# Weights in another order, so that 48 modes are summed ahead of the tail, and a tail with 32-row spectra on four row groups and pairs of banks

## The chip, the cores and the metric

The kernel runs on one core of a Trainium2 chip. The metric is the device time of one execution in microseconds (us). Every time quoted comes from runs of the state "fast" (one single look, one_group, has no known state); a few tenths of a per cent matter here, so the experiments were timed in three or five rounds beside the kernel before. A ratio is the mean time of one kernel's fast runs over the mean of the other's fast runs in the same rounds, so it is not quite the ratio of the medians that are quoted with it. All kernels of one call shared a chip and the runs of the kernel before; the experiments came in four calls, on four chips.

PE is the matmul engine, DVE the vector engine, ACT the scalar engine, POOL a fourth engine that can also add, SP the queue that issues most output transfers. A bank is one PSUM accumulator of 128 x 512 f32 sums. The clock is the part of full speed that PE was granted (1.00 or 0.50 where it matters here), the share of transfers is the mean busy share of the 16 DMA engines.

## The reference, cut to what matters

```python
# attention: 8 batches, 8 heads, 576 rows, 64 columns; heads 0-3 a local mask, 4-7 a strided one
x = attention(q, k, v)                       # [8, 576, 512]
X = np.fft.rfft(x, axis=1)                   # 64 modes are kept
Yr = einsum('bmd,mde->bme', Xr, w_r) - einsum('bmd,mde->bme', Xi, w_i)
Yi = einsum('bmd,mde->bme', Xr, w_i) + einsum('bmd,mde->bme', Xi, w_r)
y = np.fft.irfft(Y, n=S, axis=1)
u = x + y
return (u + np.maximum(u @ w_ch, 0.0)).astype(np.float32)     # out [8, 576, 512], 9.44 MB
```

Each mode has its own two 512 x 512 matrices. 64 modes of them are 134 MB in HBM and half of that in the 16-bit form in which the kernel keeps them. Every output row needs every mode: the inverse transform is a matmul whose contracted dimension is (mode, real or imaginary), 128 rows in all.

## The kernel before

The weights stream in half modes (256 of 512 input rows), in pairs of modes; one half of all 64 modes comes first, beside the attention, then the other half, beside the products with `w_ch` and the transposes.

```python
    def w_fetch(n=1):
        for _ in range(n):
            i = len(w_tiles)
            if i >= 2 * NM:
                return
            half, m = 1 - i // NM, i % NM
            if i // 2 in GUEST:
                wt = big.tile([128, 2, 4, DM], F16, tag=GUEST[i // 2], name="wt")
            else:
                wt = pw.tile([128, 2, 4, DM], F16, tag="w", name="wt")
            for ri, src in enumerate((moe_w_r, moe_w_i)):
                dst = wt[ds(64 * ri, 64)]
                rows = src[m : m + 2, ds(256 * half, 256), :].rearrange(
                    "m (p c) e -> p m (c e)", c=4
                )
                dst = dst.rearrange("p m c e -> p m (c e)")


                ones = range(2)
                if ri and not m:
                    ones = [1]
                elif i < 2 * NM - 4:
                    nc.gpsimd.dma_start(dst, rows)
                    continue
                for j in ones:
                    nc.gpsimd.dma_start(dst[:, j], rows[:, j])
            w_tiles.extend((wt[:, 0], wt[:, 1]))
```

When a group of 16 modes is complete, its spectra (`yys`, 32 rows per batch, and `zzs`, their product with `w_ch`) are copied to rows 32g to 32g+31 of a 128-row tile. Once the last group (g = 3) is there, the tail begins. It has 36 units of 128 output rows, each with a bank `v` (input of the relu) and a bank `u` (the sum), and one matmul over all 128 rows of spectra:

```python
    def rows_of(b, t, acc, spectra, fresh):
        if t < 4:
            todo = [(out_cols(t), b)]
        else:
            todo = [(ds(576, 128), b - 1), (ds(512, 128), b)]
        for i, (cols, bb) in enumerate(todo):
            nc.tensor.matmul(
                acc,
                cs["cA"][:, cols],
                spectra[bb],
                start=fresh and i == 0,
                stop=(i == len(todo) - 1),
            )
```

The units of the tail (cut):

```python
    def v_rows(i):
        b, t = units[i]
        if i not in vps:
            v_early(i)
        vp = vps.pop(i)
        rows_of(b, t, vp, zzs, False)
        if t % 2 == 0:
            n = len(rls) // 2 % 2
            rl = ptr.tile([128, 2, 576], FP, tag="xT" if n else "rl", bufs=2, name="rl")
            rls[b, t] = rls[b, t + 1] = rl[:, :, 0:DM]
        rl = rls[b, t][:, t % 2, :]
        nc.scalar.activation(out=rl, in_=vp, func=ACTF.Relu)
        if pool_adds(b, t):
            nc.gpsimd.tensor_tensor(out=rl, in0=rl, in1=x_rows(b, t), op=AluOp.add)

    def u_early(i):
        b, t = units[i]
        ups[i] = psum("u")
        if not pool_adds(b, t):
            nc.tensor.matmul(ups[i], idn, x_rows(b, t), start=True, stop=False)

    def u_rows(i):
        b, t = units[i]
        if i not in ups:
            u_early(i)
        up = ups.pop(i)
        rows_of(b, t, up, yys, pool_adds(b, t))
        if t % 2 == 0:
            osbs[b, t] = osbs[b, t + 1] = pw.tile([128, 2, DM], FP, tag="w", name="osb")
        osb = osbs[b, t]
        halves = [ds(0, 256), ds(256, 256)] if i == LAST else [slice(None)]
        for cols in halves:
            nc.vector.tensor_tensor(
                out=osb[:, t % 2, cols],
                in0=up[:, cols],
                in1=rls[b, t][:, t % 2, cols],
                op=AluOp.add,
            )
        if t == 4:
            for j in range(2):
                (nc.scalar if b == B - 1 and j else nc.sync).dma_start(
                    out[b - 1 + j, ds(512, 64), :], osb[ds(64 * j, 64), 0, :]
                )
        elif i < 2 or i >= LAST - 1:
            for j, cols in enumerate(halves):
                (nc.scalar if i == LAST and j == 0 else nc.sync).dma_start(
                    out[b, ds(128 * (t - t % 2), 256), cols].rearrange(
                        "(p i) e -> p i e", i=2
                    )[:, t % 2, :],
                    osb[:, t % 2, cols],
                )
        elif t % 2:
            nc.sync.dma_start(
                out[b, ds(128 * (t - 1), 256), :].rearrange("(p i) e -> p i e", i=2),
                osb,
            )
    ...
    for m in range(END, NM):
        mode(1, m)
        if m < END + 2:
            for w in early[3 * (m - END) : 3 * (m - END) + 3]:
                w()
        else:
            again(0 if m < NM - 6 else 4 if m < NM - 2 else 2)
    spec_last(0)
    again(3)
    v_early(2, warm)
    spec_out(3, 0, *held[0])
    done = 0
    for i in range(len(units)):
        v_rows(i)
        b, t = units[i]
        if t == 1 and b + 1 < B:
            if b + 1 == 4:
                spec_last(1)
            spec_out(3, b + 1, *held[(b + 1) // 4])
        lag = 3 if 3 < i < LAST - 3 else 2
        while done <= i - lag:
            u_rows(done)
            done += 1
    while done <= LAST:
        u_rows(done)
        done += 1
    psum_pools()
```

The softmax here doesn't subtract the row's maximum and nothing guards it: scores larger than these inputs give would overflow.

## Time and profile before

| | before |
|---|---|
| median of 4 runs | 434.88 us (433.83 to 436.02) |
| span of the profiled run | 434.2 us |
| last weight matmul ends | 394.7 us |
| first add of the tail starts, last ends | 399.7, 428.4 us |
| output transfers flow | 401.3 to 431.5 us |

The prediction below shows the page, the stretches and the groups of this profile. Two more views serve the comparison. First the timeline of PE and DVE at the start of the tail (columns: start, us, engine, line, operation, output from inputs, shape, count, and the idle time ahead of it with what ended that).

```profile
394.08 0.64 PE L547 MATMUL y<-X,wt 128*128 128x16 f16 x16
395.30 1.91 PE L887 MATMUL y<-w_ch,YT 128*128 128x512 f16 x4
399.74 0.69 DVE L929 TENSOR_TENSOR osb<-u,rl 128x512 f32<-128x512 f32 x1 [0.28 <-ACT rl L908]
```

Four 512-column matmuls take 1.91 us at 395.3; at full clock they take 1.04 us (order_alone, below). The clock reads 0.50 from 395.0 to 397.3: PE runs them at half clock. Second, a stretch of 1 us in the tail (columns: busy PE, weight load, DVE, ACT, POOL; clock; transfer share; GB/s).

```profile
403.00:404.00 1.00, 1.00 (x7) 0.41 (x6) 0.84 (x2) 1.00 (x3) 1.00 (x2) 1.00 0.00 0
```

The transfer engines stand still for this 1 us (share 0.00, as at 411 to 412) while every compute engine works, so in the kernel before the tail is bound by compute more than by transfers.

### The profile page before, as it was taken

The page shows a single profiled execution, that of the slowest core. Times are in us where ns is not written, and L with a number is a line of the kernel's source. Part 1 is how long each engine was busy: PE and PEld are TensorE (multiplying, and loading weights), DVE is VectorE, ACT ScalarE, POOL GpSimd, SP SyncE. Part 2 cuts the span into 40 slices and gives each one's busy share as a digit, 9 for nine tenths or more (in the row PEclk, how much of TensorE's full clock was granted, in tenths as well). Part 3 has the DMA queues.
Part 4 walks back from the last instruction along what each step waited for, and adds up shares of the span by engine and source line. Part 5 has one row for each costly group of instructions (what it writes and reads, how often), then busy time and mean ns, then how long its engine had stood idle before and what let it go on. Part 6 is the DMA issues. An engine that isn't in the chain of part 4 may idle for free.

```text
span 434.2 us, 12103 instructions
## 1 busy us (share of the span) xinstructions
PE 338.5 (78%) x5307; PEld 244.5 (56%) x5307; DVE 215.9 (50%) x468; ACT 187.5 (43%) x352; POOL 129.3 (30%) x208
## 2 busy tenths in 40 slices
PE   1986888779985787889885566587789798968993
PEld 1865776658864575667753344454456465643441
DVE  2888678744433243342511033355436366503894
ACT  1686678634643435444440401143215123602892
POOL 6433332322332222222222222222222221200992
PEclk9999899865985859875865569887958899988999
DMA  8999999999999999999999999999999999991787
GB/s 176 210 211 213 214 212 213 211 211 213 213 212 212 214 214 212 214 214 213 214 212 213 213 214 214 212 214 215 211 214 214 212 214 214 213 182 30 272 330 261
DMA packets 29140, 92.18 MB, mean 212 GB/s; under 512 B 4064, under 2 KB 5344, under 8 KB 29088
## 3 DMA queue, kind: packets, MB, share of 16 engines
q0 software_dynamic: 24704, 81.28, 94.4%
q1 hardware_dynamic: 3584, 9.59, 5.9%
q8 instruction: 42, 0.69, 0.6%
q10 hardware_dynamic: 800, 0.54, 0.5%
q14 instruction: 10, 0.08, 0.0%
HBM read 163.22 MB, written 9.44 MB: 398 GB/s over the span
## 4 chain that ended last, share of the span: by engine, by line
DMA 68%; PE 19%; DVE 6%; ACT 2%; issue 2%; POOL 1%; DVEq 0%; POOLq 0%
DMA wt<-in_moe_w_i_dram 51%; DMA wt<-in_moe_w_r_dram 11%; DMA ring<-in_q_dram 5%; PE y L547 2%; PE v L689 2%; DVE xb L250 2%; DVE kz L292 2%; PE u L689 2%; PE v L895 2%; PE sc L514 1%; ACT X L260 1%; PE tp L395 1%; DVE rec L249 1%; PE sc L441 1%; PE sc L353 1%
## 5 line engine op out<-in xcount | busy, mean ns | idle before, releaser
L547 PE MATMUL y<-X,wt 128*128 128x16 f16 (+1 forms) x2048 | 82.4, 192 | 61.0 <-DMA wt<-in_moe_w_i_dram 59.4
L547 PEld LDWEIGHTS <-wt 128*128 128x128 f16 (+1 forms) x2048 | 72.9, 103 | 76.5 <-issue 68.5
L196 POOL DMA_DIRECT2D wt<-in_moe_w_r_dram x62 | 36.5, 589 | 141.7 <-PE y L547 67.4
L196 POOL DMA_DIRECT2D wt<-in_moe_w_i_dram x60 | 35.4, 590 | 73.5 <-DMA wt<-in_moe_w_i_dram 61.2
L654 ACT ACTIVATE v<-sc 128x512 f16<-128x512 f32 x32 | 19.1, 597 | 69.7 <-PE sc L645 69.6
L645 PE MATMUL sc<-w_cp,xT 128*128 128x512 f16 (+1 forms) x160 | 48.2, 430 | 0.0
L471 ACT ACTIVATE PL<-sc 128x480 f16<-128x480 f32 (+1 forms) x48 | 27.3, 580 | 46.8 <-PE sc L457 46.5
L655 DVE COPY xo<-tp 128x512 f16<-128x512 f16 x32 | 22.1, 692 | 35.7 <-PE tp L653 35.6
L249 DVE RECIPROCAL rec<-av 90x4 f32<-90x4 f32 (+2 forms) x80 | 14.7, 184 | 46.2 <-PE av L486 34.8
L250 DVE TENSOR_TENSOR xb<-av,rec 90x256 f16<-90x256 f32 (+2 forms) x80 | 36.0, 450 | 2.7
L402 DVE COPY qT<-tp 128x576 f16<-128x576 f16 x16 | 12.0, 758 | 38.8 <-PE tp L395 35.9
L260 ACT ACTIVATE v<-tp 128x640 f16<-128x640 f16 (+1 forms) x24 | 19.4, 808 | 24.9 <-PE tp L429 22.1
L395 PE MATMUL tp<-cI_s,ring 64*64 64x64 f16 x864 | 26.7, 213 | 0.8 <-DVE qT L402 0.6
L360 ACT ACTIVATE PL<-sc 90x360 f16<-90x360 f32 (+1 forms) x48 | 22.7, 491 | 6.1 <-PE sc L353 5.3
L929 DVE TENSOR_TENSOR osb<-u,rl 128x512 f32<-128x512 f32 (+1 forms) x37 | 23.7, 674 | 1.8 <-PE u L689 1.1
L395 PEld LDWEIGHTS <-ring 64*64 64x64 f16 x864 | 21.1, 125 | 5.7 <-issue 2.6
L910 POOL TENSOR_TENSOR rl<-rl,xo 128x512 f32<-128x512 f32 x16 | 18.3, 1157 | 18.2 <-ACT rl L908 17.9
L441 PE MATMUL sc<-cMl_s,cI_s 128*128 128x480 f16 (+1 forms) x48 | 22.5, 468 | 1.6 <-ACT X L260 1.6
L457 PE MATMUL sc<-qT,kz 128*128 128x160 f16 (+1 forms) x160 | 22.4, 267 | 0.0
L908 ACT ACTIVATE rl<-v 128x512 f32<-128x512 f32 x36 | 20.4, 600 | 4.7 <-PE v L689 3.9
L285 PE MATMUL tp<-cI_s,ring 72*128 72x72 f16 x256 | 15.1, 206 | 9.4 <-DMA ring<-in_v_dram 7.9
L260 ACT ACTIVATE kz<-tp 64x360 f16<-64x360 f16 (+1 forms) x32 | 19.1, 595 | 7.7 <-PE tp L395 6.1
(103 smaller groups left out, 655.7 us busy)
## 6 DMA issues: line engine op xcount, KB each, us to landing
wt<-in_moe_w_r_dram POOLq DMA_DIRECT2D x62, 512.0 KB, 19.0
wt<-in_moe_w_i_dram POOLq DMA_DIRECT2D x60, 512.0 KB, 19.4
out_dram<-osb SPq DMA_DIRECT2D x14, 512.0 KB, 2.7
ring<-in_v_dram POOLq DMA_DIRECT2D x8, 288.0 KB, 13.3
ring<-in_q_dram POOLq DMA_DIRECT2D x8, 288.0 KB, 13.6
ring<-in_k_dram POOLq DMA_DIRECT2D x8, 288.0 KB, 13.5
ring<-in_v_dram POOLq DMA_DIRECT2D x3, 512.0 KB, 15.0
ring<-in_q_dram POOLq DMA_DIRECT2D x3, 512.0 KB, 14.8
```

The source lines that it names most:

```text
L196: nc.gpsimd.dma_start(dst, rows)
L250: nc.vector.tensor_tensor(out=dst, in0=val.rearrange("p h (q c) -> p h c q", c=4), in1=rec[0:n, 0:pieces] .to_broadcast((n, pieces, 64)) . ...
L260: nc.scalar.activation(out=out, in_=in_, func=ACTF.Copy)
L360: nc.scalar.activation(out=PS[0:n, ds(POFF[t], 4 * n)], in_=scp[0:n, 0 : 4 * n], func=ACTF.Exp, scale=SCALE,)
L395: nc.tensor.transpose(tp[ds(64 * hp, 64), ds(64 * i, 64)], qn[ds(64 * hp, 64), ds(64 * (9 * g + i), 64)], idn[ds(64 * hp, 64), ds(64 * hp, ...
L441: nc.tensor.matmul(scp[:, 0 : n * times].rearrange("p (h x) -> p h x", h=times), idn, mask_rows("cMl", n, times), start=True, stop=False,)
L457: nc.tensor.matmul(scp[:, ds(col, n)], kzs[par][:, hp, ds(s0, 128)], qTs[par][:, ds(s0, n)], start=False, stop=(i == len(todo) - 1),)
L471: nc.scalar.activation(out=dst, in_=src, func=ACTF.Exp, scale=SCALE)
L547: nc.tensor.matmul(yv[:, mi, e, :], wt[pr, XC[c], ds(128 * e, 128)], Xh[half][pr, c, :, :, m], start=(c == 0), stop=(c == 3),)
L645: nc.tensor.matmul(vp[pr, :], xT[:, ch, cols], w_chs["cp"][:, ch, :], start=(ch == 0), stop=(ch == 3),)
L655: nc.vector.tensor_copy(out=xo[pr].rearrange("p (h q c) -> p h q c", h=2, c=4), in_=tp[pr, 0:512].rearrange("p (h c q) -> p h q c", h=2, c=4),
L929: nc.vector.tensor_tensor(out=osb[:, t % 2, cols], in0=up[:, cols], in1=rls[b, t][:, t % 2, cols], op=AluOp.add,)
```

## The change

The intent: the tail does in 34 us what waits for the last weights, and most of it need not wait. The new order puts 24 half modes at the end of the stream: 8 of the first half (modes 56 to 63), then 16 of the second (48 to 63). So modes 0 to 47 are complete when those begin. While they stream, `renew` adds the 96 rows of those 48 modes into the kept rows `v0` and `xo`. In the tail 32 rows of spectra remain. Four 32-row matmuls can stand in four row groups of PE at once, so the tail works in items of two batches, with `v` and `u` as pairs of banks, and relu and add over 1024 columns. POOL has no part in it any more. The diff, cut to its core:

```diff
+    SPLIT1, SPLIT0 = 56, 48
+    ORDER = [(1, m) for m in range(SPLIT1)] + [(0, m) for m in range(SPLIT0)]
+    ORDER += [(1, m) for m in range(SPLIT1, NM)] + [(0, m) for m in range(SPLIT0, NM)]
-            half, m = 1 - i // NM, i % NM
+            half, m = ORDER[i]
...
-                cs["cA"][:, cols],
-                spectra[bb],
+                cs["cA"][0:96, cols],
+                spectra[bb][0:96],
...
-    NMODES = [11, 9, 8, 8, 7, 7, 7, 7]
+    psum_pools(y=2, tp=2, sc=2, av=2)
+    NMODES = [10, 8, 7, 7, 6, 6, 6, 6]
...
+    def renew(b, ts):
+        n = len(ts)
+        if n == 2:
+            v0, xo = v0s[b][:, ts[0] : ts[0] + 2], xos[b][:, ts[0] : ts[0] + 2]
+        else:
+            v0, xo = v0h[b // 2].unsqueeze(1), xoh[b // 2].unsqueeze(1)
+        vp, up = psum("v", pair=True), psum("u", pair=True)
+        for j, t in enumerate(ts):
+            nc.tensor.matmul(vp[:, j], idn, v0[:, j], start=True, stop=False)
+            rows_of(b, t, vp[:, j], zzs, False)
+        act_copy(v0, vp[:, 0:n])
+        for j, t in enumerate(ts):
+            rows_of(b, t, up[:, j], yys, True)
+        nc.vector.tensor_tensor(out=xo, in0=up[:, 0:n], in1=xo, op=AluOp.add)
...
+    def new_rows(k, acc, spectra):
+        P, t = items[k]
+        for j in range(2):
+            b = 2 * P + j
+            q = ds(32 * (b % 4), 32)
+            if t < 4:
+                o, cols = acc[:, j], out_cols(t)
+            else:
+                o, cols = acc[ds(64 * j, 64), 0], ds(576, 64)
+            nc.tensor.matmul(
+                o,
+                A3[q, cols],
+                spectra[b // 4][q],
+                start=False,
+                stop=True,
+            )
...
+    def v_done(k):
+        n = len(units_of(items[k]))
+        rl = ptr.tile([128, 2, 576], FP, tag=("xT", "rl")[k // 2 % 2], bufs=2, name="rl")
+        rls[k] = rl[:, 0:n, 0:DM]
+        nc.scalar.activation(out=rls[k], in_=vps.pop(k)[:, 0:n], func=ACTF.Relu)
...
+        osb = osbs[P]
+        nc.vector.tensor_tensor(
+            out=osb[:, :, t % 2], in0=up, in1=rls.pop(k), op=AluOp.add
+        )
+        for j in range(2):
+            dst = out[2 * P + j, ds(128 * (t - t % 2), 256), :].rearrange(
+                "(p i) e -> p i e", i=2
+            )
+            if k < 4:
+                nc.sync.dma_start(dst[:, t % 2], osb[:, j, t % 2])
+            elif t % 2:
+                nc.sync.dma_start(dst, osb[:, j])
...
+    spec_last(0, "v2")
+    new_rows(0, vps[0], zzs)
+    new_rows(0, ups[0], yys)
+    v_done(0)
+    u_done(0)
+    v_early(1)
+    new_rows(1, vps[1], zzs)
+    v_done(1)
+    spec_last(1, "u")
+    for k in range(2, LAST + 2):
+        if k <= LAST:
+            v_early(k)
+        u_early(k - 1)
+        if k <= LAST:
+            new_rows(k, vps[k], zzs)
+        new_rows(k - 1, ups[k - 1], yys)
+        if k <= LAST:
+            v_done(k)
+        u_done(k - 1)
```

## The prediction

> **What bounds the kernel now.** I read the page first: the busy slices and the queues.
>
> ```profile
> PE   1986888779985787889885566587789798968993
> DMA  8999999999999999999999999999999999991787
> GB/s 176 210 211 213 214 212 213 211 211 213 213 212 212 214 214 212 214 214 213 214 212 213 213 214 214 212 214 215 211 214 214 212 214 214 213 182 30 272 330 261
> q0 software_dynamic: 24704, 81.28, 94.4%
> ```
>
> One slice is 10.9 us. The transfers are at nine tenths and 213 GB/s (counted in the 16-bit form that lands) for 35 slices: the kernel streams 64 modes of weights and everything else hides in that. Slice 37 is nearly empty, then the rate is higher again: these are the output writes. So there are two limits in turn, the weight stream to about 392.9 us and a tail of 41 us. The chain of waits agrees on the stream.
>
> ```profile
> DMA wt<-in_moe_w_i_dram 51%; DMA wt<-in_moe_w_r_dram 11%; DMA ring<-in_q_dram 5%; PE y L547 2%; PE v L689 2%; DVE xb L250 2%; DVE kz L292 2%; PE u L689 2%; PE v L895 2%; PE sc L514 1%; ACT X L260 1%; PE tp L395 1%; DVE rec L249 1%; PE sc L441 1%; PE sc L353 1%
> ```
>
> Next the busy time by stretch (columns: length; PE, PE loads, DVE, ACT, POOL busy; granted clock; transfer share; GB/s), to see what limits the tail.
>
> ```profile
> 395.00:400.00 5.00, 4.96 (x20) 2.19 (x19) 2.08 (x6) 1.34 (x3) 0.00 (x0) 0.69 0.02 5
> 400.00:405.00 5.00, 5.00 (x25) 2.25 (x23) 4.38 (x8) 4.90 (x10) 3.82 (x4) 1.00 0.46 181
> 410.00:415.00 5.00, 5.00 (x24) 2.24 (x23) 4.61 (x8) 4.07 (x8) 3.95 (x4) 1.00 0.70 282
> 420.00:425.00 5.00, 5.00 (x25) 2.29 (x24) 4.77 (x9) 3.98 (x7) 4.26 (x4) 1.00 0.95 353
> 425.00:430.00 5.00, 2.26 (x11) 0.82 (x9) 3.29 (x6) 1.29 (x3) 1.18 (x2) 1.00 0.91 329
> ```
>
> PE and DVE are full, but the transfers too are at 0.70 to 0.95. Finer stretches of half a microsecond show the rate when the share is about 1, and where it falls.
>
> ```profile
> 403.00:403.50 0.50, 0.50 (x4) 0.21 (x3) 0.34 (x2) 0.50 (x2) 0.50 (x2) 1.00 0.00 0
> 409.50:410.00 0.50, 0.50 (x4) 0.19 (x2) 0.47 (x2) 0.25 (x1) 0.50 (x1) 1.00 1.00 410
> 422.00:422.50 0.50, 0.50 (x4) 0.21 (x3) 0.50 (x2) 0.50 (x2) 0.01 (x1) 1.00 0.92 238
> 431.00:431.50 0.50, 0.00 (x0) 0.00 (x0) 0.00 (x0) 0.00 (x0) 0.00 (x0) 1.00 0.46 162
> ```
>
> Rows of 4 KB go at 400 to 410 GB/s, so 512 KB takes 0.524 MB / 0.405 = 1.29 us. The 64-row pieces of t = 4 go at about 238: 256 KB takes 1.1 us. Output flows from 401.2 to about 431.3, 30.1 us.
>
> Last, the groups of the tail by shape give the durations.
>
> ```profile
> L929 DVE TENSOR_TENSOR osb<-u,rl 128x512 f32<-128x512 f32 x35 | 23.0, 689 | 1.8 <-PE u L689 1.1 <-ACT rl L908 0.4
> L908 ACT ACTIVATE rl<-v 128x512 f32<-128x512 f32 x36 | 20.4, 600 | 4.7 <-PE v L689 3.9
> L910 POOL TENSOR_TENSOR rl<-rl,xo 128x512 f32<-128x512 f32 x16 | 18.3, 1157 | 18.2 <-ACT rl L908 17.9
> L689 PE MATMUL v<-zz,cA_s 128*128 128x512 f16 x40 | 14.2, 379 | 0.0
> L929 DVE TENSOR_TENSOR osb<-u,rl 128x256 f32<-128x256 f32 x2 | 0.7, 415 | 0.0
> ```
>
> (379 ns is a modelled duration; the chain's steps show that one 512-column matmul follows the other after 0.216 us.)
>
> **What the Trainium skill says.** "TensorE: Matmul & The Clock Gate", Measured speedup vs the span model: four row tiles (K=32, N=512) were 3.07 times as fast as one after the other. "TensorEngine Tiling (Array Packing)", Key Properties: changing the tiling mode drains the TensorE. No 32-row matmul in the trace of before tests either one; at the change from full-array to 64-row transposes at 207.5 us starts lie 0.12 us apart where 0.03 was the step, so I take 0.1 us for a change. The first page's clock section says that the array runs at half rate after an idle window of about 3.4 us. The trace agrees: after the idle time at 381 to 384 us the steps are 0.427 us and the clock reads 0.50, against 0.216 and 1.00 in the tail. "DMA: Bandwidth & Descriptors", Issuing engines are not separate DMA queues: all share the same 16 engines, so output cannot go faster by more queues; its fabric ceiling, 435 GB/s, is just above the 410 seen.
>
> **The change, part by part.**
>
> *Order of the weights.* The same 128 half modes, the same bytes and buffers: the stream's length stays. Attention shares its stretch with 56 modes and no longer 64. A mode comes every 2.46 us (a 1 MB pair at 213 GB/s is 4.9 us), so it has 8 x 2.46 = 20 us less. PE is 82% busy at 100 to 200 us at a clock of 0.76, which at full clock is 62%; about 70% in the shorter stretch. No bound. The 24 modes at the end (59 us) gain 20 renewals, one per mode: at most 6 matmuls x 0.216 = 1.3 us, one ACT copy and one DVE add of 1024 columns. With the mode's 0.65 us PE has 1.95 us of work in 2.46 us: hidden, though not by much, and denser work keeps the clock up. The last mode still arrives near 392.9.
>
> *Start of the tail.* Before: last mode's matmuls end at 394.72, the last spectra are made from 395.3 to 397.6, first relu 399.03, first add 399.74, first output 400.46. After: the spectra copy is one 0.6 us ACT copy (before 0.37, half width), relu of two banks and add of two banks. By the slope from 256 to 512 columns, 1024 columns take 0.69 + 2 x (0.689 - 0.415) = 1.24 us on DVE, and by the same means (0.373, 0.600) 1.05 us on ACT. First add done at about 400.8, hence first data 0.3 us later, but two units and not one.
>
> *The tail's work.* 36 units become 16 double items and 4 single ones.
> - DVE: 16 x 1.24 + 4 x 0.69 = 22.6 us; before 23.0 + 0.7 for the adds, plus 8 copies of 0.42 and two casts (1.1): 28.2. A saving of 5 us.
> - POOL: 20 x 1.16 = 23 us go away; its adds lay beside other work.
> - PE, one double item: 4 identity matmuls x 0.216 = 0.86, four 32-row matmuls on four row groups 4 x 0.216 / 3.07 = 0.28, two mode changes 0.2: 1.34 us. Before, two units took 3.0 us (27.5 us of steps from 398.4 to 425.9 for 36 units, 0.76 each, is 1.53 per two without the spectra stretch of 1.1 us: about 1.5).
> - So an item comes every 1.34 to 1.4 us, limited by PE with DVE (1.24 + gaps) right behind, and a single one every 0.8. After item 0 the second spectra block and its bank wait put item 1 at about 403.5. Fourteen more doubles x 1.38 and four singles x 0.8 give 403.5 + 19.3 + 3.2 = 426.0 for the last add; before 428.44. That is 2.4 us earlier.
>
> *The transfers.* Service: 4 items in 2 KB rows at 385 GB/s (401.5 to 402 us) 4 x 1.36 = 5.4; 12 items 12 x 1.29 = 15.5; four t = 4 pairs 4 x 1.1 = 4.4: 25.3 us. Data starts 0.9 us after an add ends (before: add 400.43, data about 401.3). Items 0 to 5 are served by 410.8. Items 6 and 7 are even rows and issue nothing; item 8 is done at 412.1, so the engines idle from 410.8 to 413.0. Items 8 and 9: 413.0 to 418.2. Items 12 and 13: 418.5 to 423.7. Items 16 and 17: 424.0 to 429.2, then the two t = 4 pairs to 431.4. Before, the bulk ended at 431.3. **The 2.4 us that compute gains are lost** to 5 us of idle engines: 1.3 before item 1, 2.2 for the gap after t = 4, and gaps of 0.3; and the last 2.5 MB leave after DVE is nearly done. From the end of the bulk to the end of the span it is 2.9 us in both.
>
> **Rivals.**
> 1. *Output transfers bound the tail fully and run without gaps.* For it: share 0.95 at 420 to 425 us. Then the end is 400.8 + 0.9 + 25.3 = 427.0, plus 2.9: 429.9 against 434.2, so 4.3 us better, about 430.6 in the median. Against it: item 1's delay and the even items that issue nothing. This is also the floor; 2% (8.7 us) is out of reach while the stream ends at 392.9.
> 2. *Row groups don't run side by side, or mode changes cost more.* Four 32-row matmuls in turn are 0.86 us in place of 0.28, an item 1.92, and 14 of them put the last add near 434 and the end near 441 to 444. At a cost of 0.2 per change, an item is 1.54 and the end some 2 to 3 us later than before. Nothing in the trace of before excludes these.
> 3. *PE becomes late at the end of the stream.* Renewals at the half clock cost 6 x 0.427 = 2.6 us, above the 2.46 per mode; should PE be cold at 384 to 390, as before, it would reach the last modes up to 1 us late. Against: it is then warm at 395 to 397, where before the spectra ran at half clock (four steps of 0.43, 0.85 us lost). Sum about zero.
>
> **Range and chances.** The schedule gives 434.2 + 0.2 in the profile. An add bound by DVE alone (1.29) would give 0.8 us less than before. I weigh the schedule, that and some weight for rival 1, and say 0.6 us below before's median: 434.3. Low end 431.0, just above rival 1's floor; high end 438.5, rival 2's milder form. Faster by 2% would need 426.2 and I give 0.02; slower by 2% needs 443.6, the full rival 2: 0.06.
>
> **What would show it.** The stream's last weight matmul near 394.7 (within 1 us); the double add and relu at 1.24 and 1.05 us; adds 1.3 to 1.4 us apart; POOL empty after the stream; the last add near 426, with the transfers busy for about 5 us after it; an idle stretch of about 2 us near 411 to 413. Wrong if 32-row matmuls start 0.216 us apart, if the last weights come at another time, or if transfers with a backlog run faster than 410 GB/s.

## The result

| | before | changed |
|---|---|---|
| median of 4 runs | 434.88 us (433.83 to 436.02) | 435.56 us (435.43 to 435.87) |
| ratio, 95% interval | | 1.0026 (1.0003 to 1.0049): same within 2% |
| span of the profiled run | 434.2 us | 433.8 us |
| last weight matmul ends | 394.7 us | 396.0 us |
| first add starts, last ends | 399.7, 428.4 us | 400.2, 426.8 us |
| output transfers flow | 401.3 to 431.5 us | 402.3 to 432.0 us |

From the page of the changed kernel, the row of GB/s in 40 slices, as in the prediction:

```profile
GB/s 171 209 212 212 213 213 212 212 211 213 213 212 215 213 213 216 212 215 212 213 212 215 213 213 214 213 214 213 213 213 214 213 214 214 213 187 28 243 323 306
```

The stream of weights is as before, 213 GB/s, and so is its end. The difference is in the tail. Its groups by shape:

```profile
L958 DVE TENSOR_TENSOR osb<-u,rl 128x1024 f32<-128x1024 f32 x16 | 19.6, 1224 | 2.6 <-ACT rl L940 0.8 <-PE u L928 0.6
L940 ACT ACTIVATE rl<-v 128x1024 f32<-128x1024 f32 x16 | 16.4, 1024 | 5.8 <-PE u L928 4.2 <-PE v L928 1.6
L928 PE MATMUL v<-zz,cFl_s 32*128 32x512 f16 x32 | 6.2, 384 | 0.7 <-ACT zz L265 0.7
```

The double add takes 1.224 us where two took 2 x 0.689, and the double relu 1.024 us where two took 2 x 0.600. The 32-row matmuls (`32*128`) have taken the place of the 128-row ones. The chain that ended last, in the middle of the tail (columns: start, us, what):

```profile
415.97 0.54 PE v L908 x2
416.51 0.43 PE u L917 x2
416.94 0.32 PE v L928 x2
417.26 0.01 PE u L928 x2
```

One item is 1.30 us, all of it PE: 0.97 us for the four identity matmuls with one change of the tiling mode, 0.32 us for the four 32-row ones with the other. The add (1.224 us) fits below it with 0.07 us to spare. The timeline of DVE shows the whole tail:

```profile
400.20 1.23 DVE L958 TENSOR_TENSOR osb<-u,rl 128x1024 f32<-128x1024 f32 x1 [0.81 <-ACT rl L940]
403.16 3.96 DVE L958 TENSOR_TENSOR osb<-u,rl 128x1024 f32<-128x1024 f32 x3
408.29 0.69 DVE L947 TENSOR_TENSOR osb<-u,rl 128x512 f32<-128x512 f32 x1 [0.58 <-issue]
409.63 15.57 DVE L958 TENSOR_TENSOR osb<-u,rl 128x1024 f32<-128x1024 f32 x12 [0.64 <-PE u L928]
```

After item 0 DVE copies the second block of spectra (402.55 to 403.24, not shown), then come the items at 1.3 us: 3 in 3.96 us, 12 in 15.57. From first add to last the tail is 26.6 us where it was 28.7. What became of these 2.1 us is in the stretches:

```profile
412.00:414.00 2.00, 2.00 (x16) 0.72 (x12) 1.84 (x3) 1.61 (x2) 0.00 (x0) 1.00 0.02 5
414.00:424.00 10.00, 10.00 (x62) 3.08 (x61) 9.35 (x9) 8.03 (x9) 0.00 (x0) 1.00 0.98 392
424.00:429.00 5.00, 1.45 (x9) 0.31 (x7) 2.49 (x3) 0.78 (x2) 0.00 (x0) 0.78 1.01 402
```

For 2 us nothing is sent (share 0.02), though PE and DVE work; then the transfers run without a gap to 432, the last 5 us of it with no compute left. The adds end 1.7 us earlier than before, the transfers 0.5 us later.

**Two clocks in one comparison.** The profiled run of before is 0.4 us longer than that of the changed kernel, while the medians stand the other way by 0.7 us. A device time is about 1.75 us above the span of its own profile (changed: 435.58 and 433.8 us), so the profiled run of before was one of about 436.0 us, at the upper end of its four. Half clock at 395 us is what that profile has and the other has not; the run of the order alone comes back to it. That this is the cause of the longer run is likely, not shown: single runs have no trace beyond the profiled one.

### The profile page after: what moved, and what is told of

Same layout as the page of the kernel before. It is cut to its first block, busy times and chain, and to the rows that moved or that the text cites. A ratio compares the mean times of both kernels' runs of the same rounds, so it can differ in the third digit from the quotient of the medians.

```text
span 433.8 us, 12282 instructions
## 1 busy us (share of the span) xinstructions
PE 347.5 (80%) x5424; PEld 241.5 (56%) x5424; DVE 239.1 (55%) x463; ACT 204.1 (47%) x355; POOL 106.6 (25%) x188
## 5 line engine op out<-in xcount | busy, mean ns | idle before, releaser
L552 PEld LDWEIGHTS <-wt 128*128 128x128 f16 (+1 forms) x2048 | 73.3, 101 | 42.4 <-issue 31.8
L650 PE MATMUL sc<-w_cp,xT 128*128 128x512 f16 (+1 forms) x160 | 46.7, 419 | 0.0
L476 ACT ACTIVATE PL<-sc 128x480 f16<-128x480 f32 (+1 forms) x48 | 27.3, 579 | 33.6 <-PE sc L462 33.4
L407 DVE COPY qT<-tp 128x576 f16<-128x576 f16 x16 | 12.0, 758 | 36.6 <-PE tp L400 33.6
L882 DVE TENSOR_TENSOR xo<-u,xo 128x1024 f16<-128x1024 f32 x16 | 19.6, 1225 | 15.2 <-PE u L690 15.1
L400 PE MATMUL tp<-cI_s,ring 64*64 64x64 f16 x864 | 25.0, 204 | 2.0 <-issue 1.2
L265 ACT ACTIVATE v<-v 128x1024 f16<-128x1024 f32 x16 | 16.4, 1024 | 17.8 <-PE v L690 17.8
L446 PE MATMUL sc<-cMl_s,cI_s 128*128 128x480 f16 (+1 forms) x48 | 21.2, 441 | 3.3 <-ACT X L265 1.6
L400 PEld LDWEIGHTS <-ring 64*64 64x64 f16 x864 | 19.5, 117 | 6.9 <-issue 3.2
L519 PEld LDWEIGHTS <-xb 108*128 108x128 f16 (+2 forms) x176 | 15.3, 106 | 12.8 <-DVE xb L255 8.2
L940 ACT ACTIVATE rl<-v 128x1024 f32<-128x1024 f32 (+1 forms) x20 | 18.8, 939 | 7.2 <-PE u L928 5.4
L462 PEld LDWEIGHTS <-kz 128*128 128x128 f16 x160 | 15.3, 111 | 11.6 <-issue 8.1
```

What stands on the lines that cost most here:

```text
L265: nc.scalar.activation(out=out, in_=in_, func=ACTF.Copy)
L400: nc.tensor.transpose(tp[ds(64 * hp, 64), ds(64 * i, 64)], qn[ds(64 * hp, 64), ds(64 * (9 * g + i), 64)], idn[ds(64 * hp, 64), ds(64 * hp, ...
L446: nc.tensor.matmul(scp[:, 0 : n * times].rearrange("p (h x) -> p h x", h=times), idn, mask_rows("cMl", n, times), start=True, stop=False,)
L476: nc.scalar.activation(out=dst, in_=src, func=ACTF.Exp, scale=SCALE)
L552: nc.tensor.matmul(yv[:, mi, e, :], wt[pr, XC[c], ds(128 * e, 128)], Xh[half][pr, c, :, :, m], start=(c == 0), stop=(c == 3),)
L650: nc.tensor.matmul(vp[pr, :], xT[:, ch, cols], w_chs["cp"][:, ch, :], start=(ch == 0), stop=(ch == 3),)
```

## The experiments

Twelve kernels ran, all in the state "fast" but for the single look, whose state is unknown. The table has the ratio to the kernel before of the same rounds, and from each trace the end of the last weight matmul, the start of the first add of the tail, and what is left from there to the end of the span. The last column leaves out what came before the first add, and so most of what the clock at the last spectra costs. It is not quite free of it: of the four runs with the old tail, the two at half clock there (before, loads_before) have 34.5, the two at full clock (order_alone, whole_before) 33.7 and 33.9. From the last weight matmul to the end it is 39.5 us in the first two and 37.4 and 37.6 in the others. So less than 0.8 us of the last column says little by itself.

| run | median us | ratio (95%) | last weights | first add | first add to end |
|---|---|---|---|---|---|
| before | 434.88 | | 394.7 | 399.7 | 34.5 |
| changed | 435.56 | 1.0026 (1.0003-1.0049) | 396.0 | 400.2 | 33.6 |
| one_group | 446.22 (one run) | | 397.0 | 402.0 | 42.4 |
| rows_at_once | 435.75 | 1.0027 (1.0015-1.0040) | 396.2 | 400.3 | 33.6 |
| spec_late | 435.99 | 1.0020 (1.0007-1.0032) | 395.8 | 400.0 | 33.9 |
| order_alone | 434.68 | 0.9992 (0.9982-1.0002) | 395.3 | 398.9 | 33.7 |
| rows_all | 434.28 | 0.9993 (0.9976-1.0011) | 396.2 | 402.0 | 32.4 |
| rows_all_spec_late | 434.99 | 0.9993 (0.9974-1.0012) | 396.4 | 400.6 | 31.6 |
| loads_after | 436.05 | 1.0027 (1.0014-1.0041) | 397.1 | 402.9 | 33.6 |
| loads_before | 435.81 | 1.0009 (0.9998-1.0021) | 394.9 | 399.9 | 34.5 |
| tail_best | 432.40 | 0.9942 (0.9921-0.9963) | 395.8 | 399.5 | 30.9 |
| whole_before | 435.91 | 1.0024 (1.0013-1.0035) | 396.2 | 399.8 | 33.9 |
| whole_best | 434.02 | 0.9975 (0.9964-0.9985) | 397.8 | 401.4 | 31.0 |
| no_renew | 437.88 | 1.0066 (1.0036-1.0095) | 395.8 | 400.7 | 34.6 |

The theory (A): the tail of the changed kernel ends with its output transfers; an idle stretch of theirs is lost for good, so compute that gets faster gains nothing while items of even rows send nothing. The rival (B): PE and DVE at 1.30 us an item set the end.

### The four row groups

```diff
-            q = ds(32 * (b % 4), 32)
+            q = ds(0, 32)
```

> All four 32-row matmuls of an item read row group 0 (a wrong result on purpose for three of four batches; same instructions, waits and transfers). Theory A (the four row groups work side by side, and that is what makes an item 1.30 us): the four run in turn, an item becomes about 0.86 + 0.86 + 0.1 to 0.2 = 1.9 us, the last add comes near 435 us in place of 426.7 and the span is about 440 us (6 us longer). Rival (an item is bound by the DVE add of 1.225 us or by something else, and row groups matter little): the span stays within 1 us of 433.8.

Measured: 446.22 us, span 444.4, 10.6 us longer. Below are four 32-row matmuls and the two matmuls after them, in the timeline of PE, first of the changed kernel, then of this run.

```profile
415.58 0.39 PE L928 MATMUL v<-zz,cFl_s 32*128 32x512 f16 x2
415.59 0.39 PE L928 MATMUL u<-yy,cFl_s 32*128 32x512 f16 x2
415.91 0.61 PE L908 MATMUL v<-v,cI_s 128*128 128x512 f16 x2
```

```profile
422.55 0.60 PE L928 MATMUL v<-zz,cFl_s 32*128 32x512 f16 x2
422.99 0.59 PE L928 MATMUL u<-yy,cFl_s 32*128 32x512 f16 x2
423.51 0.60 PE L908 MATMUL v<-v,cI_s 128*128 128x512 f16 x2
```

On four row groups all four start within 0.02 us and PE goes on 0.33 us after the first; on one group they take 0.96 us, 2.9 times as long, the change of mode included. ("TensorE: Matmul & The Clock Gate", Measured speedup vs the span model, has 3.07 times for four row tiles: it agrees.) An item becomes 1.93 us, as expected, and the DVE add then waits some 0.7 us for each. The end is 4.4 us later than was expected of it. Of this 2.7 us is the last add, which ends at 437.7 and not 435, most of it since the first add came 1.8 us later than in the changed kernel; the rest is that the expectation left 5 us from the last add to the end, where this run takes 6.7 and the changed kernel 7.1. The transfers drain between the items (nothing is sent at 416 to 419, 426 to 427 and 433 to 435 us), so at this rate PE sets the end, as rival B has it. The side-by-side work of the row groups is shown; the changed kernel lives from being just fast enough.

The run was within the tolerance of the comparison with the reference, though three batches in four had wrong spectra of 16 modes. no_renew, below, passed too, though its sums lack 48 of the 64 modes. So that comparison sees little of the modes at all, and is no proof that the sums over them are right in any of these kernels.

### The idle stretch before the last transfers

```diff
-            if k < 4:
+            if k < 10:
                 nc.sync.dma_start(dst[:, t % 2], osb[:, j, t % 2])
```

> The first ten double items, not only the first four, send each 2 KB row as soon as its add is done, so the transfer engines have work in the stretch from 412 to 414 us in which they stood still. Theory A (the end is set by the output transfers, which from 414 us run without a gap, so idle stretches before it are lost for good): the idle stretch of 2.0 us goes away, ten transfers of 512 KB in 2 KB rows cost some 0.3 us more, and the end comes 1.5 to 2 us earlier (ratio to before about 0.998). Rival B (the tail is bound by PE and DVE at 1.30 us an item): no change, within 0.3 us of the changed kernel.

Measured: 1.0027, the changed kernel's own ratio. As the number stands, A has missed. The stretches of this run tell why:

```profile
412.00:414.00 2.00, 2.00 (x15) 0.72 (x12) 1.84 (x3) 1.48 (x2) 0.00 (x0) 1.00 0.99 353
418.00:419.50 1.50, 1.50 (x10) 0.41 (x8) 1.43 (x2) 1.23 (x2) 0.00 (x0) 1.00 0.00 0
```

The stretch at 412 is busy now (share 0.99), and a new idle one lies at 418 to 419.5: items 10 and 11 are even and send nothing, and transfers have no backlog by then. The stretch had only moved. My expectation forgot that transfers (1.29 to 1.36 us an item) are hardly slower than adds (1.30 us), so no backlog builds up that could bridge two silent items. All items must send at once:

```diff
-            if k < 4:
+            if k <= LAST:
```

> Every double item sends its 2 KB rows as soon as its add is done, so no item makes the transfer engines wait for its odd partner (the run with the first ten items showed the idle stretch only moved, from 412-414 to 418-419.6 us, and the end with it stayed). Theory A (the end is the last idle stretch plus the transfers after it): no idle stretch after 407 us; one 512 KB transfer of 1.36 us per item of 1.30 us follows the adds closely, and after the last add of a double item at 425.2 us there is about one such transfer and the two t = 4 pairs to send: transfers end near 430.3 in place of 432.1, 1.5 to 2 us earlier than the changed kernel, ratio to before about 0.998. Rival (the smaller rows cost what the closed gap gives): the same time as the changed kernel, within 0.5 us.

Measured: 0.9993 against 1.0026 and 1.0027 of the two before it, 0.3% or 1.4 us less. It ran in another call on another chip, so only the ratios can be compared: the interval of rows_all (up to 1.0011) overlaps that of the changed kernel (from 1.0003) and lies clear of that of rows_at_once (from 1.0015). The trace agrees: from the first add to the end of the span 32.4 us in place of 33.6, which loads_after, below, also has, with the tail of the changed kernel and at half clock like this run.

```profile
414.00:418.00 4.00, 4.00 (x26) 1.32 (x25) 3.79 (x4) 3.18 (x4) 0.00 (x0) 1.00 0.99 380
418.00:424.00 6.00, 6.00 (x40) 1.83 (x37) 5.71 (x5) 4.88 (x5) 0.00 (x0) 1.00 0.99 381
```

No idle stretch is left here, at 381 GB/s in 2 KB rows in place of 402 in 4 KB rows. The expected 1.5 to 2 us came as 1.2 in the trace and 1.4 in the times, just below it. This profiled run itself was one of the longer ones (436.38 us, state fast): PE came to the last spectra at half clock.

### The second block of spectra, later

```diff
-    spec_last(1, "u")
     for k in range(2, LAST + 2):
+        if k == 9:
+            spec_last(1, "u")
```

> The second block of last spectra (8 matmuls, an ACT copy, a DVE copy, one bank pair) is made ahead of the tenth item and not between the first two. Theory A: item 1 is done about 1.5 us earlier and the first transfers with it, but the gap at 412 us is only moved or gets longer, since items 6 and 7 still send nothing; the block of 1.3 us on PE comes just before item 8 sends its 1 MB, so the continuous run of transfers starts at the same time: the span is within 0.5 us of 433.8. Rival B (compute bound): the same total of work, so no change either; a gain of over 1 us would speak for a third cause, the start of the tail.

Measured: 1.0020, no change from 1.0026, as both theories had it: item 1 is done at 403.2 and not 404.4 us, and transfers then stand still from 411 to 414. Together with all rows sent at once:

> As the run in which every item sends at once, and the second block of last spectra ahead of the tenth item. Theory A (transfers and adds now both go at 1.3 to 1.36 us an item, so an early start of the transfers counts): item 1 is sent 1.2 us earlier, the transfers are about 1 us ahead when the block comes and lose little of it; the end comes 0.3 to 1.0 us before the run without this move. Rival (adds alone set the end, their sum is unchanged): the same as without the move, within 0.2 us.

Measured: 0.9993 in both, so the timed runs show no gain; from first add to end 31.6 against 32.4 us in the traces, which is within what was expected of A. With intervals of 0.18% (0.8 us) either way the two can't be told apart by time, so A and its rival both stay open, and the block was left in its later place.

### The order of weights alone

The kernel before, its tail and all, with the new order and the split of the attention that goes with it (cut: the loop over the modes follows the order too).

```diff
+    ORDER = [(1, m) for m in range(SPLIT1)] + [(0, m) for m in range(SPLIT0)]
+    ORDER += [(1, m) for m in range(SPLIT1, NM)] + [(0, m) for m in range(SPLIT0, NM)]
...
-            half, m = 1 - i // NM, i % NM
+            half, m = ORDER[i]
...
-    NMODES = [11, 9, 8, 8, 7, 7, 7, 7]
+    NMODES = [10, 8, 7, 7, 6, 6, 6, 6]
```

> The kernel before with the new order of weights alone: its tail, with 128-row spectra, single banks and POOL adds, is untouched, and no sums are renewed. Theory A (the order itself is free, the stream of weights ends when its bytes are through): the last weight matmul ends within 0.5 us of 394.7 and the time is the same as before, ratio 0.999 to 1.001. Rival C (the order makes the stream end later, by the shorter stretch of the local attention, and this is the 1.3 us by which the changed kernel's last weights came late): the last weight matmul ends near 396 us and the time is 1 us longer, ratio about 1.003.

Measured: 0.9992 (0.9982 to 1.0002): the order costs nothing that shows. The last weights are done at 395.3 us, 0.6 later than in the profile of before and just outside the expected 0.5; the kernel before with its last loads whole, which is the same program up to there, was 0.6 us later already at mode 54 (377.81 against 377.22), so this much is the spread of one profile to the next. What this trace has that the other has not is the full clock:

```profile
394.61 0.64 PE L550 MATMUL y<-X,wt 128*128 128x16 f16 x16 [0.17 <-DMA wt<-in_moe_w_i_dram]
395.63 1.04 PE L892 MATMUL y<-w_ch,YT 128*128 128x512 f16 x4
```

The four products take 1.04 us, not 1.91, and the first add starts 3.7 us after the last weight matmul, not 5.0: 1.3 us of the time of either kernel hang on whether PE is at full clock there. That would explain why the profile of before, at half clock there, was longer than its median. And with the old tail this run needs 33.7 us from the first add to the end, where the changed kernel needs 33.6: the new form of the tail has bought nothing by itself.

### The end of the weight stream

In both kernels the last 5 us of the stream, 388 to 393 us, run at about half the share. The last two pairs of modes are loaded as single modes, real, real, imaginary, imaginary, and each kind goes to one half of the partitions. The edit puts them in turn:

```diff
-                for j in ones:
-                    nc.gpsimd.dma_start(dst[:, j], rows[:, j])
+                if i >= 2 * NM - 4:
+                    last.append((dst, rows))
+                    continue
...
+            for j in range(2):
+                for dst, rows in last:
+                    nc.gpsimd.dma_start(dst[:, j], rows[:, j])
```

> The changed kernel with the last eight single weight loads in the order real, imaginary, real, imaginary (before: both real, then both imaginary ones of a pair). In both kernels the last 4.5 to 6 us of the stream run at 98 to 115 GB/s with a share of about 0.5, since only loads to one half of the partitions are left. Theory D (those loads use half of the transfer engines): with both halves busy to the end the last weights come 1 to 2 us earlier, and the time with them, ratio to before about 0.998 to 1.000. Rival (the last loads are held by their late issue, one every 2.4 us, not by the halves): the last weights come within 0.3 us of the same time.

> The kernel before with the same order of its last eight single loads, so that a better version is compared with both. Theory D: 1 to 2 us less than before, ratio 0.995 to 0.998. Rival: the same as before within 0.3 us.

Measured: 1.0027 and 1.0009, so no gain in either; the slow end stays, at 94 to 127 GB/s from 389 us on. Theory D as I put it has fallen. The rival, late issue of small loads, was tested by loading the last two pairs whole (`elif i < 2 * NM - 4:` becomes `else:`), in the kernel before and in the version of the next section:

> The kernel before with its last two pairs of modes loaded as whole pairs like all others (four loads of 512 KB and not eight of 256 KB). The run with the eight loads in another order left the slow end of the stream as it was (102 to 115 GB/s from 388 to 393 us), so the halves of the partitions are not its cause. Theory E (loads are issued one per 2.4 us, each waiting for an older one to land, so a load of half the size halves the rate): the stream keeps 213 GB/s to its end and the last weights come 1.5 to 2.5 us earlier, the time with them: ratio 0.995 to 0.997. Rival F (something else thins out the end of the stream): last weights within 0.5 us, or later since the first mode of a pair waits for both: ratio 0.999 to 1.002.

> Both of these together, on the changed kernel. Theories A and E: the sum of the two, though PE works off its renewals until about 392.7 us and takes up some of the earlier weights: 431.5 to 432.5 us, ratio to before 0.991 to 0.994. If E fails, as the run of the tail alone, 0.995 to 0.997.

Measured: 1.0024 and 0.9975 (against 0.9942 with single loads). A stretch of whole_before, with the same columns as above:

```profile
388.00:393.50 5.50, 5.11 (x43) 2.10 (x41) 0.56 (x1) 0.00 (x0) 0.00 (x0) 0.50 0.55 111
```

The last load was issued at 376.5 us, 11 us before this stretch, and was of full size; the share was still 1.04 at 384 to 388 us, and falls to 0.55 all the same: theory E has fallen too. At 111 GB/s for 5.5 us the rest is 0.6 MB, about one load of 512 KB. That would fit one half of the transfer engines being a whole load behind the other, but no run here shows the engines one by one, so the cause stays open. It is the same in both kernels and no part of the change.

### The late last weights of the changed kernel

> The changed kernel without its 20 renewals beside the last 24 modes (a wrong result on purpose: the sums lack 48 modes; the tail, the order of weights and the transfers are as they were). The last mode starts at 395.2 to 395.8 us in all traces with renewals, at 394.1 to 394.6 in the three traces with the old tail. Theory G (the renewals make PE free the weight buffers later, so the last loads land later): without them the last mode starts at 394.0 to 394.7. Rival (the order of weights or the banks make it late): it stays at 395.2 to 395.8. The end may be some 1 us later all the same, if PE then comes to the last spectra at half clock.

The edit replaces both `late.append(... renew ...)` by `pass`. Measured: 1.0066, 437.88 us: with less work the kernel is slower. The timeline of PE at the last two modes:

```profile
393.00 0.64 PE L552 MATMUL y<-X,wt 128*128 128x16 f16 x16 [3.14 <-DMA wt<-in_moe_w_i_dram]
393.48 1.02 PE L908 MATMUL v<-v,cI_s 128*128 128x512 f16 x2
```

PE stands idle until the weights of mode 62 land at 393.0 (394.0 in the changed kernel, though 393.1 to 393.4 in four of its variants), then does its four early matmuls at half clock (1.67 us; 0.86 at full) and is late for mode 63 by itself. Mode 63 starts at 395.15 us; by the expected number, 394.0 to 394.7, theory G has missed, and the run does not settle it, since the clock came in. What it shows is that without renewals the clock stays at 0.50 from 380 to 396 us, where the changed kernel has 1.00. Renewals are no guarantee: with all of them, rows_all and loads_after fall to half clock at about 396 and 397 us, with no idle time of PE above 0.9 us in the 10 us before. It also ran 1.5 us longer in the profile with a first add only 0.5 us later; where the other 1 us went I have not found. Why mode 63 comes at 395.2 to 395.8 us in most traces with renewals, and not in all as the expectation says (396.3 in one_group, 396.5 in loads_after, 397.1 in whole_best), but at 394.1 to 394.6 in three of the four with the old tail (395.5 in the fourth), stays open.

### A version that beats both

On top of rows_all_spec_late: the two products of the first block in banks of their own, so that the ACT and DVE copies need not wait for each other; two own-row matmuls that stood between the last weights and that block put behind it; fillers ahead of each of the last two modes.

```diff
+        if i == NL - 1:
+            ups[0] = psum("u", pair=True)
+            u_own(0)
+            u_own(0)
...
-    v_own(0)
     yctx.close()
...
-    spec_last(0, "v2")
+    zl, yl = psum("zl"), psum("yl")
+    spec_mm(3, 0, yl, zl)
+    v_own(0)
+    act_copy(zzs[0], zl)
+    nc.vector.tensor_copy(out=yys[0], in_=yl)
+    sctx.close()
...
```

> The run with all rows sent at once and the late second block, with three more changes at the start of the tail: the two products of the first block in two banks of two tiles, so that the ACT copy does not wait for the identity product and the DVE copy not for the ACT copy; the two own-rows matmuls that stood between the last weights and that block put behind it; and the fillers spread so that PE has work in front of each of the last two modes. Theory A (with gap-free transfers the end follows the first add): the first add 0.7 to 1.0 us earlier, the end as well, fewer runs with the spectra at half clock; 433.0 to 433.8 us, ratio to before 0.995 to 0.997. Rival (the start of the tail is not what the end follows, adds have slack): the same as that run, ratio 0.999.

Measured: 432.40 us (431.98 to 433.49), ratio 0.9942 (0.9921 to 0.9963) to before, more than was expected. First the two copies and the first add, then the tail:

```profile
397.34 0.60 ACT L265 ACTIVATE zz<-zl 128x512 f16<-128x512 f32 x1 [4.69 <-PE zl L675]
397.51 0.69 DVE L1008 CAST yy<-yl 128x512 f16<-128x512 f32 x1 [1.35 <-PE yl L671]
399.47 1.23 DVE L962 TENSOR_TENSOR osb<-u,rl 128x1024 f32<-128x1024 f32 x1 [1.26 <-ACT rl L944]
```

```profile
414.00:424.00 10.00, 9.76 (x61) 2.98 (x59) 9.41 (x8) 7.70 (x9) 0.00 (x0) 1.00 1.01 382
```

The copies run side by side (in the changed kernel 398.07 and 398.70, one after the other), the first add starts 3.6 us after the last weight matmul and not 4.2, and transfers are over at 429 and not 432. All of its seven fast runs lie below the lowest of before in those rounds (433.81), while rows_all has runs from 433.2 to 437.3. (Seven are few: most kernels have 22 on record, and the record does not say why this one has not.) That the fillers are what took away the slow ones fits the trace, whose spectra run at full clock, but the fillers were not tried by themselves. Theory A is right in its direction: against rows_all_spec_late the first add starts 1.1 us earlier (0.6 of it since the last weights came earlier) and the span ends 1.8 us earlier. Where the other 0.7 us came from, and which of the three changes gave what, was not tested.

## Why the prediction was right

The prediction was "the same", 434.3 us, in 431.0 to 438.5; it came as 435.56: the class and the reason held, while the number is 1.3 us off, with a gain of 0.6 us forecast and a loss of 0.7 measured. By its steps:

- **The stream's length stays.** Right for the order (order_alone, 0.9992). The last weight matmul was put within 1 us of 394.7 and came at 396.0: a miss of 0.3 us beyond that, open as to cause.
- **First add done at about 400.8.** It was done at 401.4. The later weights cost 1.3 us; of this 0.7 came back since PE was at full clock for the spectra, which rival 3 had named.
- **Durations.** Double add 1.24, measured 1.224; double relu 1.05, measured 1.024.
- **PE per double item 1.34 us, items every 1.34 to 1.4.** Measured 1.30. (Beside it stands a slip: two units of before did not take 3.0 us but the 1.5 that the same sentence works out; nothing rests on it.) The four 32-row matmuls with the change back to the full array took 0.33 us, the other change 0.1: the two terms of 0.28 and 0.2 were together a little large. PE is the limit with DVE right behind, as stated: the chain has no gap and no DVE in it.
- **Single items every 0.8 us.** This term was too small: 1.26 us (407.03 to 408.29) where a single one stands between doubles, 0.94 at the end. A neighbour of 64 columns beside one of 128 keeps the two pairs of 32-row matmuls apart: at 405.05 and 405.39, in place of together.
- **The last add at 426.0.** 426.8. Item 1 was done 0.9 us later than the 403.5 put down (404.4); after it fourteen doubles at 1.30 took 1.1 us less and four singles 1.0 us more. That the sum is so near is partly luck.
- **Idle transfers from 410.8 to 413.0 after the t = 4 items.** Measured at 412.1 to 414.3. This was the step on which "no gain" rested. rows_all, which has no silent items, is better by 1.2 us (trace, from the first add to the end) to 1.4 us (times), with the reservation made there.
- **End of the bulk 431.4.** 432.0.
- **Rivals.** Rival 2 (row groups in turn, end at 441 to 444) is what one_group made happen, at 444.4. Rival 1's floor, 429.9 us of span, is nearly reached by tail_best with 430.4; so most of that gain was there to be had. Sending every item at once and a better start of the tail brought it; their shares were not separated.

What the prediction did not have is that the comparison itself hung on the clock: it took the profile of before as the typical run, and that profile held half clock worth 1.3 us up to the first add.

## What to carry to other kernels

When the last stage ends in output transfers whose rate is about that of the compute, look for the moments at which nothing is sent: if the transfers after it run without a gap to the end, such a moment is added to the end, and faster compute only makes it longer. Send each piece as soon as it is done even if its rows are then half as long, and bring the first piece forward. Before reading a difference of 1 us from two profiles, check that PE ran at the same clock in both where the chain passes.

## What the Trainium skill lacked or had wrong

- "TensorEngine Tiling (Array Packing)", Key Properties, says that a change of the tiling mode drains the TensorE but gives no time. Here a change costs about 0.1 us (0.31 us from the start of the last 128-row matmul to the first 32-row one, where the step is 0.216), and tiles of 32 rows with 64 and with 128 columns side by side did not start together: 0.34 us apart.
- "TensorE: Matmul & The Clock Gate", What's actually happening, has half clock follow an idle window of about 3.4 us. Here it came without one: in rows_all PE was idle for at most 0.9 us at a time after 385 us and busy for 2.15 of the 3.42 us up to 395.87, and the clock fell from 1.00 to 0.50 there; rows_at_once, busy for 2.06 of the 3.40 us up to 395.80, kept 1.00. The page also has the ramp penalty at under 1% of a span. That agrees (1.3 us, 0.3%), but it does not say that so much can be as large as the effect of a change.
- "SBUF — State Buffer", "Can I just issue two DMAs to hit both halves?", says that two DMAs, one at partition 0 and one at partition 64, reach only 6% more than one and serialize, and its table has 64 partitions at an asymptote of about 218 GB/s. Here the t = 4 pieces, issued one behind the other for the two halves of the partitions, went at 238 GB/s in the kernel before (422.0 to 422.5 us) and at 279 to 311 in the changed one (430.5 to 431.5 us), at a share of 0.92 to 0.99: more than that page gives one half, so the two did overlap; from 128 partitions at once it was 402 for 4 KB and 381 for 2 KB rows.
